# Loading the key cache in 4 KB rows, and the projection weights in pieces, in a decode attention kernel

## Chip, cores and metric

The kernel runs on one core of one Trainium2 chip. The metric is device time in microseconds (us), the median over several executions. Only one core works in every run here, so nothing below says what happens when a second core uses the same memory.

How ratios are computed: a ratio is the mean time of one kernel's runs over the mean of the runs of the kernel before, taken in the same rounds on the same chip. It is therefore not quite the ratio of the medians that are quoted beside it.

Names: TensorE is PE in the profile, its weight load is PEld, VectorE is DVE, ScalarE is ACT, and the engine that only issues transfers is SP. HBM is the memory off the core, SBUF the memory that the engines read, PSUM where TensorE writes. A "row" of a load means bytes that lie back to back both in HBM and in one SBUF partition; the load moves each as one packet.

## The reference

One decode step of attention with grouped heads, over the last W = 512 of 2048 cached keys. B = 32 batch rows, one query each, D = 512, Hq = 32 query heads, Hkv = 8 key/value groups, so 4 query heads per group (rep), head size Dh = 128, everything in bf16.

```python
q = (x @ wq).reshape(B, 1, 32, 128).transpose(0, 2, 1, 3)
k = repeat(k_cache[:, :, -512:, :], 4, axis=1)   # k_cache, v_cache: [32, 8, 2048, 128]
v = repeat(v_cache[:, :, -512:, :], 4, axis=1)
p = softmax(einsum("bhqd,bhkd->bhqk", q, k) * 128 ** -0.5)
o = einsum("bhqk,bhkd->bhqd", p, v)
out = o.transpose(0, 2, 1, 3).reshape(B, 1, 4096) @ wo
```

The part of K that is used is 33.5 MB, that of V as much; wq and wo are 4.2 MB each. Nothing is used twice, so some 75.5 MB must come from HBM once.

## The kernel before

For each of the 8 groups, K of 32 batch rows is loaded and transposed on TensorE (by a matmul with an identity), since the scores need Dh on the partitions. The scores of all 32 batch rows are accumulated into one PSUM tile of 128 rows (32 batch rows x 4 heads) by 512 keys. Then come the softmax, four transposes of P, and the PV matmuls, which are delayed by one group. All loads go through one queue, in program order: K of the next group first, then V of this one.

```python
def issue_k(g):                       # issue_v is the same with v_cache
    kgs = []
    for cb in range(NBCH):            # 4 loads of 8 batch rows, 1 MB each
        kg = kg_pool.tile([P, BCH, NC, Dh], bf16, name="kg", tag="kg")
        dma.dma_start(
            out=kg,
            in_=k_cache[cb * BCH : (cb + 1) * BCH, g, w0:Sk, :].rearrange(
                "b (p c) d -> p b c d", p=P),   # 4 keys (1 KB) per partition and batch row
        )
...
for g in range(Hkv):
    kgs = kg_next
    if g + 1 < Hkv:
        kg_next = issue_k(g + 1)
    vgs = issue_v(g)
    if g == 0:
        wq_h1 = ...; dma.dma_start(out=wq_h1, in_=wq_v[:, :, HHALF * Dh : HD])        # 2 MB
        wo_sb = ...; dma.dma_start(out=wo_sb, in_=wo.rearrange("(h d) n -> d h n", d=P))  # 4 MB
    if g == 2:
        q_proj_heads(wq_h1, HHALF)     # 64 matmuls
    if g >= 3:
        emit_proj(g - 2)               # output projection of an earlier group
    ...
    for b in range(B):
        for c in range(NC):            # NC = 4 transposes of 128 keys
            nc.tensor.matmul(ps_kt[:, c, :], lhsT=kg[:, b % BCH, c, :], rhs=ident, ...)
        ...                            # copy ps_kt to kt, in turn on VectorE and ScalarE
    for b in range(B):
        nc.tensor.matmul(ps_s, lhsT=qp[:, b, :], rhs=kts[b].rearrange("p c pp -> p (c pp)"), ...)
    ...                                # max, exp with sum, reciprocal
    nc.vector.tensor_scalar_mul(out=p_tile, in0=p_tile, scalar1=rs)
    for c in range(NC):
        nc.tensor.transpose(ps_pT[:, c, :], p_tile[:, c, :], ident)
    nc.scalar.copy(out=pT, in_=ps_pT)
    if pending is not None:
        do_pv(*pending)                # 128 matmuls of 4 columns: V stationary, pT moving
    pending = (g, vgs, pT)
do_pv(*pending)
emit_proj(Hkv)
```

## Time and profile before

The median was 230.23 us in four runs (229.79 to 230.33). The profiled span is 228.4 us.

| what | value |
|---|---|
| DMA row of the page | full from the second slice to the third from the end |
| rate in most slices | 345 to 350 GB/s |
| packets under 2 KB | 70,800 of 71,848 |
| one group in TensorE's timeline | 24.1 us |
| wait for the last chunk of V ends | 221.85 us |

From the profile page of the kernel before: the span in 40 slices of 5.7 us. "PEclk" is the clock granted to TensorE and "DMA" the busy share of the 16 DMA engines, both in tenths; "GB/s" is what they moved.

```profile
PEclk9999999985558996799769985999599958996555
DMA  6999999999999999999999999999999999999940
GB/s 192 375 349 349 348 348 348 361 388 350 348 349 348 348 349 348 347 348 348 348 347 346 349 348 348 347 348 346 346 347 350 345 348 349 349 343 345 347 153 6
```

The DMA row is full all along, and the rate stands at one value, about 348 GB/s. It is higher in slices 2, 8 and 9 only, which are the ones with wq, whose rows are 4 KB. The sum 75.5 MB / 348 GB/s is 217 us: the stream of loads is the time, apart from a start and a tail.

From the timeline of the kernel before, TensorE only. The columns are start, length, what ran, how often, and in brackets the idle time before it and what ended that.

```profile
63.55 1.86 PE L118 MATMUL ps_out<-wo_sb,oT_all 128*32 128x512 bf16 x4 [10.14 <-DMA wo_sb<-in_wo_dram]
...
66.55 2.40 PE L201 MATMUL ps_kt<-ident,kg 128*128 128x128 bf16 x20 [1.14 <-DMA kg<-in_k_cache_dram]
...
90.83 2.40 PE L201 MATMUL ps_kt<-ident,kg 128*128 128x128 bf16 x20
...
107.83 1.75 PE L159 MATMUL ps_oT<-pT,vg 128*128 128x4 bf16 x64
110.52 0.38 PE L247 MATMUL ps_pT<-ident,p_tile 128*128 128x128 bf16 x4 [0.94 <-DVE p_tile L243]
...
114.89 1.36 PE L201 MATMUL ps_kt<-ident,kg 128*128 128x128 bf16 x11
...
221.85 1.02 PE L159 MATMUL ps_oT<-pT,vg 128*128 128x4 bf16 x32 [1.79 <-DMA vg<-in_v_cache_dram]
```

TensorE stood for 10.14 us because it needed wo, whose 4 MB sit in the queue behind group 0's V; only at 66.55 us did it begin group 2's transposes. Not needing wo would not have helped by itself: group 2's K lies behind wo in the queue, and after the projection TensorE waits another 1.14 us for it. It was wo's place in the queue that held group 2 up. From there a group takes 24.1 us (114.89 − 90.83), and in it the P transposes wait 0.94 us for the softmax. A group's K and V at 348 GB/s take 24.1 us too, so TensorE and the stream are nearly tied. At the end TensorE waits for the last V chunk until 221.85 us; the last PV matmuls, the last projection, a copy and the store make the tail.

Groups of instructions of the kernel before: busy time and mean length in ns, then the idle time before them.

```profile
L217 PE MATMUL ps_s<-kt,qp 128*128 128x512 bf16 x256 | 76.4, 385 | 0.0
...
L243 DVE TENSOR_SCALAR p_tile<-p_tile,rs 128x512 bf16<-128x512 bf16 x8 | 2.8, 352 | 0.2
```

The scores matmul takes 385 ns and the softmax scaling 352 ns. The view of waits adds that the P transposes wait 6.3 us in total for the scaling.

### The profile page before, as it was taken

What the parts mean: (1) busy time and instruction counts of PE and PEld (TensorE: products, weight loads), DVE (VectorE), ACT (ScalarE), POOL (GpSimd) and SP (SyncE); (2) the same over time, 40 slices, a digit from 0 to 9 for tenths busy, and PEclk for the clock granted to TensorE, in tenths of its full rate; (3) what the DMA queues carried; (4) which work ended last, traced back from release to release, by engine and by line L of the source; (5) the groups of instructions that cost most, each with busy time, mean ns of one, the idle gap of its engine ahead of it and who ended that gap; (6) DMA issues with size and microseconds to landing.
All of it is one profiled execution on the core that took longest, in us unless ns stands there. A gap on an engine that the chain in (4) does not pass through costs nothing.

```text
span 228.4 us, 5681 instructions
## 1 busy us (share of the span) xinstructions
PE 183.4 (80%) x2500; PEld 131.0 (57%) x2500; DVE 106.8 (47%) x205; ACT 86.9 (38%) x153; POOL 0.7 (0%) x6
## 2 busy tenths in 40 slices
PE   0389979983069997999799969998999979995633
PEld 0377657563037765876677556765677557765330
DVE  3068488431026831784258523872188317841001
ACT  2047467410016731573247521761167316732000
POOL 1000000000000000000000000000000000000000
PEclk9999999985558996799769985999599958996555
DMA  6999999999999999999999999999999999999940
GB/s 192 375 349 349 348 348 348 361 388 350 348 349 348 348 349 348 347 348 348 348 347 346 349 348 348 347 348 346 346 347 350 345 348 349 349 343 345 347 153 6
DMA packets 71848, 75.92 MB, mean 332 GB/s; under 512 B 1104, under 2 KB 70800, under 8 KB 71824
## 3 DMA queue, kind: packets, MB, share of 16 engines
q1 hardware_dynamic: 71824, 75.57, 103.3%
q8 instruction: 19, 0.31, 0.6%
q14 instruction: 5, 0.04, 0.1%
HBM read 75.53 MB, written 0.03 MB: 331 GB/s over the span
## 4 chain that ended last, share of the span: by engine, by line
DMA 39%; PE 33%; SPq 20%; ACT 3%; DVE 3%; issue 1%; ACTq 0%
DMA vg<-in_v_cache_dram 21%; SPq L145 17%; PE ps_kt L201 16%; DMA kg<-in_k_cache_dram 15%; PE ps_s L217 10%; PE ps_oT L159 4%; SPq L132 3%; PE ps_out L118 2%; DMA wq_h<-in_wq_dram 2%; ACT kt L212 2%; ACT p_tile L233 1%; DVE rmax L226 1%; PE ps_pT L247 1%; DVE p_tile L243 0%; DVE oT_all L166 0%
## 5 line engine op out<-in xcount | busy, mean ns | idle before, releaser
L210 DVE CAST kt<-ps_kt 128x512 bf16<-128x512 f32 x128 | 87.4, 691 | 44.1 <-PE ps_kt L201 40.6
L212 ACT CAST kt<-ps_kt 128x512 bf16<-128x512 f32 x128 | 74.9, 586 | 80.9 <-PE ps_kt L201 75.8
L201 PE MATMUL ps_kt<-ident,kg 128*128 128x128 bf16 x1024 | 94.3, 233 | 4.7 <-DMA kg<-in_k_cache_dram 2.3
L201 PEld LDWEIGHTS <-kg 128*128 128x128 bf16 x1024 | 77.3, 105 | 34.3 <-issue 9.5
L217 PE MATMUL ps_s<-kt,qp 128*128 128x512 bf16 x256 | 76.4, 385 | 0.0
L159 PE MATMUL ps_oT<-pT,vg 128*128 128x4 bf16 x1024 | 29.9, 165 | 8.6 <-DMA vg<-in_v_cache_dram 8.5
L159 PEld LDWEIGHTS <-vg 128*128 128x128 bf16 x1024 | 29.1, 99 | 11.8 <-DMA vg<-in_v_cache_dram 9.9
L217 PEld LDWEIGHTS <-qp 128*128 128x128 bf16 x256 | 24.3, 99 | 12.9
L118 PE MATMUL ps_out<-wo_sb,oT_all 128*32 128x512 bf16 x32 | 15.1, 626 | 12.8 <-DMA wo_sb<-in_wo_dram 10.1
L226 DVE TENSOR_REDUCE rmax<-ps_s 128x1 f32<-128x512 f32 x8 | 5.5, 691 | 25.0 <-PE ps_s L217 25.0
L233 ACT ACTIVATE p_tile<-ps_s,nbias 128x512 bf16<-128x512 f32 x8 | 5.5, 688 | 29.6 <-DVE nbias L230 29.6
L166 DVE CAST oT_all<-ps_oT 128x128 bf16<-128x128 f32 x8 | 2.3, 292 | 30.7 <-PE ps_oT L159 30.7
L118 PEld LDWEIGHTS <-oT_all 128*32 128x32 bf16 x32 | 3.5, 128 | 17.9 <-issue 14.5
L92 PE MATMUL ps_q<-xT,wq_h 128*128 128x32 bf16 x128 | 3.8, 188 | 6.8 <-DMA wq_h<-in_wq_dram 6.8
L247 PE MATMUL ps_pT<-ident,p_tile 128*128 128x128 bf16 x32 | 3.9, 259 | 6.3 <-DVE p_tile L243 6.3
L249 ACT COPY pT<-ps_pT 128x512 bf16<-128x512 bf16 x8 | 4.7, 587 | 10.3 <-PE ps_pT L247 10.3
L92 PEld LDWEIGHTS <-wq_h 128*128 128x128 bf16 x128 | 3.6, 104 | 7.2 <-DMA wq_h<-in_wq_dram 7.2
L100 DVE CAST qT<-ps_q 128x512 bf16<-128x512 f32 x2 | 1.4, 692 | 11.1 <-PE ps_q L92 11.1
L247 PEld LDWEIGHTS <-p_tile 128*128 128x128 bf16 x32 | 2.4, 111 | 6.8 <-ACT p_tile L233 6.0
L194 DVE COPY qp<-qT 128x32 bf16<-128x32 bf16 x32 | 4.3, 229 | 0.0
L242 DVE RECIPROCAL rs<-rsum 128x1 f32<-128x1 f32 x8 | 1.3, 162 | 4.7 <-ACT p_tile L233 4.7
L243 DVE TENSOR_SCALAR p_tile<-p_tile,rs 128x512 bf16<-128x512 bf16 x8 | 2.8, 352 | 0.2
(14 smaller groups left out, 8.0 us busy)
## 6 DMA issues: line engine op xcount, KB each, us to landing
kg<-in_k_cache_dram SPq DMA_DIRECT2D x32, 1024.0 KB, 11.8
vg<-in_v_cache_dram SPq DMA_DIRECT2D x32, 1024.0 KB, 12.0
wq_h<-in_wq_dram SPq DMA_DIRECT2D x2, 2048.0 KB, 11.0
wo_sb<-in_wo_dram SPq DMA_DIRECT2D x1, 4096.0 KB, 23.4
x_sb<-in_x_dram SPq DMA_DIRECT2D x1, 32.0 KB, 1.7
out_dram<-out_sb SPq DMA_DIRECT2D x1, 32.0 KB, 1.5
```

The source lines that it names most:

```text
L92: nc.tensor.matmul(ps_q[:, hh, :], lhsT=wq_half[:, kc, hl * Dh : (hl + 1) * Dh], rhs=xT[:, kc, :], start=(kc == 0), stop=(kc == KC - 1),)
L118: nc.tensor.matmul(ps_out, lhsT=oT_all[:, h, :], rhs=wo_sb[:, h, :], start=(next_proj[0] == 0), stop=(next_proj[0] == Hq - 1),)
L132: dma.dma_start(out=kg, in_=k_cache[cb * BCH : (cb + 1) * BCH, g, w0:Sk, :].rearrange("b (p c) d -> p b c d", p=P),)
L145: dma.dma_start(out=vg, in_=v_cache[cb * BCH : (cb + 1) * BCH, g, w0:Sk, :].rearrange("b (p c) d -> p b c d", p=P),)
L159: nc.tensor.matmul(ps_oT[:, b * rep : (b + 1) * rep], lhsT=vg[:, b % BCH, c, :], rhs=pT[:, c, b * rep : (b + 1) * rep], start=(c == 0), st ...
L201: nc.tensor.matmul(ps_kt[:, c, :], lhsT=kg[:, b % BCH, c, :], rhs=ident, start=True, stop=True,)
L210: nc.vector.tensor_copy(out=kt, in_=ps_kt)
L212: nc.scalar.copy(out=kt, in_=ps_kt)
L217: nc.tensor.matmul(ps_s, lhsT=qp[:, b, :], rhs=kts[b].rearrange("p c pp -> p (c pp)"), start=(b == 0), stop=(b == B - 1),)
L226: nc.vector.tensor_reduce(out=rmax, in_=ps_s, axis=mybir.AxisListType.X, op=mybir.AluOpType.max)
L233: nc.scalar.activation(out=p_tile.rearrange("r c pp -> r (c pp)"), in_=ps_s, func=AF.Exp, bias=nbias, scale=scale, accum_out=rsum,)
L247: nc.tensor.transpose(ps_pT[:, c, :], p_tile[:, c, :], ident)
```

## The change

It has two intents. The first is longer rows: K is loaded so that a partition holds 16 consecutive keys of one batch row (4 KB) instead of 4 keys (1 KB). A batch row then fills only 32 partitions, so four batch rows share a 512 KB load. Partition n = 4p + b holds keys 16p to 16p + 15 of batch row b. To sort this out again, the transposes use a permutation, `perm`, in place of the identity, and the scores matmul reads its columns in runs of 32 elements (64 bytes). The order of the keys in the scores changes, while V keeps its own layout with 1 KB rows; so the softmax scaling also reorders the columns, with a strided read. The second intent is that TensorE should not wait for weights: the q projection is cut into 16 matmuls per group, and wo comes in eight 512 KB pieces, each queued behind the V of its group.

```diff
+    QB = 4  # batch rows that share the 128 partitions of a K load
+    CQ = NC * QB  # keys (back to back in HBM) per partition: rows of 4 KB
+    perm = const.tile([P, P], bf16, name="perm")
+    nc.vector.tensor_copy(
+        out=perm.rearrange("k (b p) -> k b p", b=QB),
+        in_=ident.rearrange("k (p b) -> k b p", b=QB),
+    )
...  (issue_k)
-            kg = kg_pool.tile([P, BCH, NC, Dh], bf16, name="kg", tag="kg")
-            dma.dma_start(
-                out=kg,
-                in_=k_cache[cb * BCH : (cb + 1) * BCH, g, w0:Sk, :].rearrange(
-                    "b (p c) d -> p b c d", p=P
-                ),
-            )
+            kg = kg_pool.tile([P, BCH // QB, CQ, Dh], bf16, name="kg", tag="kg")
+            for q in range(BCH // QB):
+                b0 = cb * BCH + q * QB
+                kv = k_cache[b0 : b0 + QB, g, w0:Sk, :].rearrange(
+                    "b (p c) d -> p b (c d)", c=CQ
+                )
+                dma.dma_start(
+                    out=kg[:, q].rearrange("p c d -> p (c d)"), in_=kv
+                )
...  (group loop)
+        if g + n_wq_init < Hkv and g % GW == 0:
+            load_wq_wide((g + n_wq_init) // GW)       # 2 MB, 4 KB rows as before
         vgs = issue_v(g)
-        if g == 0:
-            wq_h1 = ...  (2 MB)
-            wo_sb = ...  (4 MB)
-        if g == 2:
-            q_proj_heads(wq_h1, HHALF)
-        if g >= 3:
-            emit_proj(g - 2)
+        wo_pieces[g] = load_wo_piece(g)               # 512 KB
+        if g + 2 < Hkv:
+            q_proj_piece(g + 2, wq_pieces.pop(g + 2)) # 16 matmuls
...  (transposes: rhs=perm instead of rhs=ident)
...  (scores)
-                rhs=kts[b].rearrange("p c pp -> p (c pp)"),
+                rhs=kts[b // QB].rearrange("d c (b p) -> d c b p", b=QB)[:, :, b % QB, :],
...  (softmax scaling)
-        nc.vector.tensor_scalar_mul(out=p_tile, in0=p_tile, scalar1=rs)
+        p_v = work.tile([P, NC, P], bf16, name="p_v", tag="p_v")
+        nc.vector.tensor_scalar_mul(
+            out=p_v.rearrange("r c (p m) -> r c p m", m=QB),
+            in0=p_tile.rearrange("r k n -> r (k n)").rearrange(
+                "r (m c p) -> r c p m", m=QB, c=NC
+            ),
+            scalar1=rs,
+        )
...  (after PV)
             do_pv(*pending)
+            emit_proj(pg, wo_pieces.pop(pg))
```

More of the change, by code (lines that the diff above doesn't have):

```diff
@@ L44 @@
     NBCH = B // BCH
-    HHALF = Hq // 2
-    assert Hkv * rep == Hq and (Hkv // 2) * rep == HHALF
+    QB = 4
+    CQ = NC * QB
+    assert Hkv * rep == Hq
     dma = nc.sync
     const = ctx.enter_context(tc.tile_pool(name="const", bufs=1))
-    wq_pool = ctx.enter_context(tc.tile_pool(name="wq_pool", bufs=1))
-    wo_pool = ctx.enter_context(tc.tile_pool(name="wo_pool", bufs=1))
+    wq_pool = ctx.enter_context(tc.tile_pool(name="wq_pool", bufs=2))
+    wo_pool = ctx.enter_context(tc.tile_pool(name="wo_pool", bufs=4))
     work = ctx.enter_context(tc.tile_pool(name="work", bufs=2))
     kg_pool = ctx.enter_context(tc.tile_pool(name="kg", bufs=6))
-    kt_pool = ctx.enter_context(tc.tile_pool(name="kt", bufs=20))
+    kt_pool = ctx.enter_context(tc.tile_pool(name="kt", bufs=6))
     v_pool = ctx.enter_context(tc.tile_pool(name="v", bufs=2 * NBCH))
@@ L66 @@
     make_identity(nc, ident)
+    perm = const.tile([P, P], bf16, name="perm")
[3 more added lines that the diff above has]
+    )
     x_sb = const.tile([B, D], bf16, name="x_sb")
     dma.dma_start(out=x_sb, in_=x[:, 0, :])
-    wq_v = wq.rearrange("(kc p) n -> p kc n", p=P)
-    wq_h0 = wq_pool.tile([P, KC, HHALF * Dh], bf16, name="wq_h0", tag="wq")
-    dma.dma_start(out=wq_h0, in_=wq_v[:, :, 0 : HHALF * Dh])
     ps_xT = psum_t.tile([P, KC, B], bf16, name="ps_xT", tag="ps_t")
@@ L81, with load_wq_wide, q_proj_piece, load_wo_piece @@
     nc.vector.tensor_copy(out=xT, in_=ps_xT)
+    wq_v = wq.rearrange("(kc p) n -> p kc n", p=P)
+    wo_v = wo.rearrange("(h d) n -> d h n", d=P)
     qT = const.tile([P, Hq, B], bf16, name="qT")
-    HB = 16
-    def q_proj_heads(wq_half, h_start):
-        for hb in range(HHALF // HB):
-            ps_q = psum_s.tile([P, HB, B], fp32, name="ps_q", tag="ps_s")
-            for hh in range(HB):
-                hl = hb * HB + hh
-                for kc in range(KC):
-                    nc.tensor.matmul(
-                        ps_q[:, hh, :],
-                        lhsT=wq_half[:, kc, hl * Dh : (hl + 1) * Dh],
-                        rhs=xT[:, kc, :],
-                        start=(kc == 0),
-                        stop=(kc == KC - 1),
-                    )
-            h0 = h_start + hb * HB
-            nc.vector.tensor_copy(out=qT[:, h0 : h0 + HB, :], in_=ps_q)
-    q_proj_heads(wq_h0, 0)
+    GW = 4
+    def load_wq_wide(w):
+        t = wq_pool.tile([P, KC, GW * rep * Dh], bf16, name="wq_w", tag="wq_w")
+        dma.dma_start(
+            out=t, in_=wq_v[:, :, w * GW * rep * Dh : (w + 1) * GW * rep * Dh]
+        )
+        for i in range(GW):
+            wq_pieces[w * GW + i] = t[:, :, i * rep * Dh : (i + 1) * rep * Dh]
+    def q_proj_piece(g, wq_p):
+        ps_q = psum_s.tile([P, rep, B], fp32, name="ps_q", tag="ps_s")
+        for j in range(rep):
+            for kc in range(KC):
+                nc.tensor.matmul(
+                    ps_q[:, j, :],
+                    lhsT=wq_p[:, kc, j * Dh : (j + 1) * Dh],
+                    rhs=xT[:, kc, :],
+                    start=(kc == 0),
+                    stop=(kc == KC - 1),
+                )
+        nc.vector.tensor_copy(out=qT[:, rep * g : rep * (g + 1), :], in_=ps_q)
+    def load_wo_piece(g):
+        t = wo_pool.tile([P, rep, D], bf16, name="wo_p", tag="wo_p")
+        dma.dma_start(out=t, in_=wo_v[:, g * rep : (g + 1) * rep, :])
+        return t
     oT_all = const.tile([P, Hq, B], bf16, name="oT_all")
@@ L109, with emit_proj @@
     ps_out = psum_out.tile([B, D], fp32, name="ps_out", tag="ps_out")
-    wo_sb = None
-    proj_done = [False] * Hq
     next_proj = [0]
-    def emit_proj(upto_g):
-        for h in range(Hq):
-            if h // rep < upto_g and not proj_done[h]:
-                nc.tensor.matmul(
-                    ps_out,
-                    lhsT=oT_all[:, h, :],
-                    rhs=wo_sb[:, h, :],
-                    start=(next_proj[0] == 0),
-                    stop=(next_proj[0] == Hq - 1),
-                )
-                proj_done[h] = True
-                next_proj[0] += 1
+    def emit_proj(g, wo_p):
+        for j in range(rep):
+            h = rep * g + j
+            nc.tensor.matmul(
+                ps_out,
+                lhsT=oT_all[:, h, :],
+                rhs=wo_p[:, j, :],
+                start=(next_proj[0] == 0),
+                stop=(next_proj[0] == Hq - 1),
+            )
+            next_proj[0] += 1
     def issue_k(g):
@@ L130, in issue_k @@
         for cb in range(NBCH):
-            kg = kg_pool.tile([P, BCH, NC, Dh], bf16, name="kg", tag="kg")
-            dma.dma_start(
-                out=kg,
-                in_=k_cache[cb * BCH : (cb + 1) * BCH, g, w0:Sk, :].rearrange(
-                    "b (p c) d -> p b c d", p=P
-                ),
-            )
+            kg = kg_pool.tile([P, BCH // QB, CQ, Dh], bf16, name="kg", tag="kg")
[3 more added lines that the diff above has]
+                    "b (p c) d -> p b (c d)", c=CQ
+                )
+                dma.dma_start(
+                    out=kg[:, q].rearrange("p c d -> p (c d)"), in_=kv
+                )
             kgs.append(kg)
@@ L169, in do_pv @@
         )
+    WQ_AHEAD = 2
+    n_wq_init = 2 + WQ_AHEAD
+    wq_pieces = {}
+    for g in range(n_wq_init):
+        if g % GW == 0:
+            load_wq_wide(g // GW)
+    for g in range(2):
+        q_proj_piece(g, wq_pieces.pop(g))
     kg_next = issue_k(0)
+    wo_pieces = {}
     pending = None
@@ L176 @@
             kg_next = issue_k(g + 1)
+        if g + n_wq_init < Hkv and g % GW == 0:
+            load_wq_wide((g + n_wq_init) // GW)
         vgs = issue_v(g)
-        if g == 0:
-            wq_h1 = wq_pool.tile([P, KC, HHALF * Dh], bf16, name="wq_h1", tag="wq")
-            dma.dma_start(out=wq_h1, in_=wq_v[:, :, HHALF * Dh : HD])
-            wo_sb = wo_pool.tile([P, Hq, D], bf16, name="wo_sb", tag="wo")
-            dma.dma_start(out=wo_sb, in_=wo.rearrange("(h d) n -> d h n", d=P))
-        if g == 2:
-            q_proj_heads(wq_h1, HHALF)
-        if g >= 3:
-            emit_proj(g - 2)
+        wo_pieces[g] = load_wo_piece(g)
+        if g + 2 < Hkv:
+            q_proj_piece(g + 2, wq_pieces.pop(g + 2))
         for j in range(rep):
@@ L196 @@
         kts = []
-        for b in range(B):
-            kg = kgs[b // BCH]
-            ps_kt = psum_kt.tile([P, NC, P], fp32, name="ps_kt", tag="ps_kt")
-            for c in range(NC):
-                nc.tensor.matmul(
-                    ps_kt[:, c, :],
-                    lhsT=kg[:, b % BCH, c, :],
-                    rhs=ident,
-                    start=True,
-                    stop=True,
-                )
-            kt = kt_pool.tile([P, NC, P], bf16, name="kt", tag="kt")
-            if b % 2 == 0:
-                nc.vector.tensor_copy(out=kt, in_=ps_kt)
-            else:
-                nc.scalar.copy(out=kt, in_=ps_kt)
+        for t in range(B // QB):
+            kg = kgs[t * QB // BCH]
+            kt = kt_pool.tile([P, CQ, P], bf16, name="kt", tag="kt")
+            for i in range(QB):
+                ps_kt = psum_kt.tile([P, NC, P], fp32, name="ps_kt", tag="ps_kt")
+                for c in range(NC):
+                    nc.tensor.matmul(
+                        ps_kt[:, c, :],
+                        lhsT=kg[:, t % (BCH // QB), i * NC + c, :],
+                        rhs=perm,
+                        start=True,
+                        stop=True,
+                    )
+                dst = kt[:, i * NC : (i + 1) * NC, :]
+                if i % 2 == 0:
+                    nc.vector.tensor_copy(out=dst, in_=ps_kt)
+                else:
+                    nc.scalar.copy(out=dst, in_=ps_kt)
             kts.append(kt)
@@ L219 @@
                 lhsT=qp[:, b, :],
-                rhs=kts[b].rearrange("p c pp -> p (c pp)"),
+                rhs=kts[b // QB].rearrange("d c (b p) -> d c b p", b=QB)[
+                    :, :, b % QB, :
+                ],
                 start=(b == 0),
@@ L242 @@
         nc.vector.reciprocal(out=rs, in_=rsum)
-        nc.vector.tensor_scalar_mul(out=p_tile, in0=p_tile, scalar1=rs)
+        p_v = work.tile([P, NC, P], bf16, name="p_v", tag="p_v")
[5 more added lines that the diff above has]
+            scalar1=rs,
+        )
         ps_pT = psum_t.tile([P, NC, P], bf16, name="ps_pT", tag="ps_t")
         for c in range(NC):
-            nc.tensor.transpose(ps_pT[:, c, :], p_tile[:, c, :], ident)
+            nc.tensor.transpose(
+                ps_pT[:, c, :],
+                p_v[:, c, :],
+                ident,
+            )
         pT = work.tile([P, NC, P], bf16, name="pT", tag="pT")
@@ L251 @@
         if pending is not None:
+            pg = pending[0]
             do_pv(*pending)
+            emit_proj(pg, wo_pieces.pop(pg))
         pending = (g, vgs, pT)
+    pg = pending[0]
     do_pv(*pending)
-    emit_proj(Hkv)
+    emit_proj(pg, wo_pieces.pop(pg))
+    assert next_proj[0] == Hq
     out_sb = work.tile([B, D], bf16, name="out_sb", tag="out_sb")
```

## The prediction

> **What bounds the kernel now.** The page's DMA row is full in nearly every slice, at 345 to 350 GB/s; 70,800 of 71,848 packets are under 2 KB. The queue's 75.5 MB take 217 us of the 228.4 us span, so the DMA stream bounds. TensorE is almost tied: in its timeline one group takes 24.1 us from 90.8 to 114.9 us (17 us of transposes and scores, the rest softmax wait, PV and output projection), with no wait for a DMA in it; a group's K plus V, 8.39 MB, takes 24.1 us at 348 GB/s. Earlier TensorE lost 10.1 us waiting for the 4 MB wo (waits view), so group 2 started only at 66.55 us.
>
> **What the change does.** K goes from 1 KB to 4 KB rows; V and wo stay at 1 KB, wq at 4 KB. In the DMA records 1 KB packets take 51 ns, 4 KB ones (wq alone) 159 ns, median. Binned by time, 1 KB rows run at 348 GB/s, and the two bins with wq alone at 407 to 410. The Trainium skill, "DMA: Bandwidth & Descriptors", section "iDMA fabric", has 408.7 GB/s for a lone load stream of 4 KiB rows: they agree. So K's 33.5 MB goes from 96.4 to 82.2 us: 14.2 us less. The last wo piece now queues behind the last V chunk, which lands 1.5 us sooner for that. Off the stream's end: about 15.7 us.
>
> TensorE gains too: no wait for wo, no block of 64 projection matmuls waiting for wq. Group 2 should start near 52 us. Added per group: 16 projection matmuls (0.5 us), and the softmax scaling with a strided read, which should lose its fast rate (352 to about 690 ns, as the 512-column casts take), seen as a longer wait of the P transposes. The scores matmul reads its moving operand in runs of 64 bytes. "SBUF — State Buffer", section on the DMA port swizzle, says consecutive accesses to one 16-byte line run at full bandwidth, so I expect 385 ns unchanged; no run so far shows it.
>
> **Critical path.** From 52 us, six groups of 24.5 us end TensorE's loop near 199 us. The stream lands the last V near 206 us. So it still ends last, by some 6 us, and all of the saving counts. Buffers keep some 20 us of loads ahead. Tail from the last V: 6.5 us, as now. Span about 212.7; the measured time lies 1.8 us above it: **214.5 us**. Range 210 to 221. Chances: faster by over 2% 0.91, within 2% 0.07, slower 0.02.
>
> **What would show each step right.** DMA rate about 400 or more where K moves, 348 where V moves; packets near 48,000; a K packet near 160 ns. Group 2's transposes start near 52 us; no long wait for wo. The scores matmul stays at 385 ns; the scaling rises to 600 to 700 ns. DMA row full until about 206 us; the last PV still waits for V.
>
> **What would make it wrong.** (a) The four batch rows of one K load lie 4 MB apart; if that slows HBM, K gains less (at 380 GB/s only 8 us). (b) If the strided scores read is slower, TensorE takes over: above about 25.5 us a group it bounds the kernel; half rate would add 7 us a group and make it slower than now. (c) The issuing queue waits for TensorE to free K buffers; with TensorE tied, the stream may starve and its row show gaps.

## The result, and the profile after

The changed kernel is correct and takes **214.33 us** (median of 8 runs, 214.19 to 214.59; the kernel before in the same rounds 230.03). The ratio is 0.9319, with an interval of 0.931 to 0.9328. The span fell from 228.4 to 212.7 us.

From the profile page after:

```profile
DMA  5999999999999999999999999999999999999950
GB/s 173 418 410 410 408 407 371 348 358 404 401 350 351 385 407 368 348 358 407 399 347 349 384 406 372 346 359 406 392 352 349 384 406 372 337 343 348 347 189 6
DMA packets 47897, 75.92 MB, mean 357 GB/s; under 512 B 1729, under 2 KB 38657, under 8 KB 47873
```

The rate now has two levels. It is 404 to 418 GB/s in slices where K or wq moves alone and near 348 where V moves alone (down to 337 late in the run), with mixed slices between, and the DMA row is still full throughout.

From the view of chosen windows, first of the kernel before, then of the changed one. The columns are the stretch, its length, the busy time (and count) of PE, PEld, DVE, ACT and POOL, the granted clock, the DMA share, and GB/s. The share can exceed 1, so it is read here only as "full".

```profile
10.00:20.00 10.00, 8.86 (x114) 7.03 (x111) 6.73 (x14) 4.57 (x8) 0.00 (x0) 1.00 1.09 351
...
88.00:94.00 6.00, 5.62 (x55) 3.78 (x52) 2.37 (x4) 1.17 (x2) 0.00 (x0) 0.50 1.10 348
```

```profile
10.00:20.00 10.00, 9.37 (x103) 7.55 (x100) 6.82 (x16) 4.59 (x8) 0.00 (x0) 1.00 1.03 409
36.00:48.00 12.00, 11.99 (x150) 8.01 (x148) 7.35 (x14) 5.90 (x11) 0.00 (x0) 1.00 1.10 353
```

The same ten microseconds, 10 to 20, carry K at 351 GB/s before and at 409 after; V, at 36 to 48 us, still moves at 353. In the DMA records of the trace a 1 KB packet takes 51.4 ns on average before, and after it the 4 KB packets have a median of 161 ns and a mean of 164.7 ns.

TensorE's timeline after:

```profile
52.03 1.89 PE L128 MATMUL ps_out<-wo_p,oT_all 128*32 128x512 bf16 x4 [0.38 <-DVE oT_all L177]
53.85 2.83 PE L222 MATMUL ps_kt<-perm,kg 128*128 128x128 bf16 x28
...
70.05 0.94 PE L170 MATMUL ps_oT<-pT,vg 128*128 128x4 bf16 x32
70.85 0.55 PE L103 MATMUL ps_q<-xT,wq_w 128*128 128x32 bf16 x16
...
72.94 0.40 PE L279 MATMUL ps_pT<-ident,p_v 128*128 128x128 bf16 x4 [0.75 <-DVE p_v L269]
...
75.31 1.60 PE L128 MATMUL ps_out<-wo_p,oT_all 128*32 128x512 bf16 x4 [0.38 <-DVE oT_all L177]
...
143.63 0.40 PE L279 MATMUL ps_pT<-ident,p_v 128*128 128x128 bf16 x4 [1.15 <-DVE p_v L269]
...
194.39 1.87 PE L128 MATMUL ps_out<-wo_p,oT_all 128*32 128x512 bf16 x4 [0.42 <-DMA wo_p<-in_wo_dram]
...
206.10 1.02 PE L170 MATMUL ps_oT<-pT,vg 128*128 128x4 bf16 x32 [1.77 <-DMA vg<-in_v_cache_dram]
```

Group 2's transposes start at 53.85 us instead of 66.55, and no wait for wo is over 0.42 us. The projection lines show a group's length, 75.31 − 52.03 = 23.3 us; those of the later groups are up to 23.7, and the last is 24.7 with a wait of 0.79 us for V in it. TensorE finishes the projection of group 6 at 196.3 us and then meets the remaining V chunks one by one: the last wait ends at 206.10 us instead of 221.85. Those 15.75 us are the whole gain (the span fell by 15.7 us); the tail from there is 6.6 us in both kernels.

Groups of instructions after, answering to those shown before:

```profile
L239 PE MATMUL ps_s<-kt,qp 128*128 128x512 bf16 x256 | 74.3, 382 | 0.0
...
L269 DVE TENSOR_SCALAR p_v<-p_tile,rs 128x512 bf16<-128x512 bf16 x8 | 5.2, 650 | 0.2
```

The scores matmul with 64-byte runs takes 382 ns against 385. The scaling takes 650 ns instead of 352, yet the P transposes wait 6.4 us in total against 6.3. The timeline shows why: in the first four of seven groups the 16 matmuls of the q projection (at 70.85 us) run while the softmax is at work, and the wait is 0.75 us. The last three have no q projection left, and there it is 1.08 to 1.15 us, longer than the 0.94 of before.

### The profile page after: what moved, and what is told of

It is laid out like the page before. It is cut to its first block, busy times and chain, and to the rows that moved or that the text cites. A ratio compares the mean times of both kernels' runs of the same rounds, so it can differ in the third digit from the quotient of the medians.

```text
span 212.7 us, 5631 instructions
## 1 busy us (share of the span) xinstructions
PE 181.5 (85%) x2500; PEld 130.7 (61%) x2500; DVE 109.0 (51%) x212; ACT 86.8 (41%) x153; POOL 0.7 (0%) x6
## 2 busy tenths in 40 slices
DMA packets 47897, 75.92 MB, mean 357 GB/s; under 512 B 1729, under 2 KB 38657, under 8 KB 47873
## 4 chain that ended last, share of the span: by engine, by line
PE 35%; DMA 31%; SPq 26%; DVE 4%; ACT 2%; issue 1%
SPq L156 20%; PE ps_kt L222 17%; DMA kg<-in_k_cache_dram 16%; PE ps_s L239 12%; DMA vg<-in_v_cache_dram 12%; SPq L114 4%; DMA wq_w<-in_wq_dram 4%; PE ps_out L128 3%; SPq L146 2%; PE ps_oT L170 2%; ACT p_tile L257 1%; DVE kt L231 1%; DVE rmax L250 1%; PE ps_q L103 1%; DVE p_v L269 1%
## 5 line engine op out<-in xcount | busy, mean ns | idle before, releaser
L231 DVE CAST kt<-ps_kt 128x512 bf16<-128x512 f32 x128 | 86.5, 690 | 31.7 <-PE ps_kt L222 28.1
L222 PE MATMUL ps_kt<-perm,kg 128*128 128x128 bf16 x1024 | 94.1, 233 | 1.9 <-ACT kt L233 0.9
L239 PE MATMUL ps_s<-kt,qp 128*128 128x512 bf16 x256 | 74.3, 382 | 0.0
L128 PE MATMUL ps_out<-wo_p,oT_all 128*32 128x512 bf16 x32 | 14.8, 615 | 3.1 <-DVE oT_all L177 2.7
L103 PE MATMUL ps_q<-xT,wq_w 128*128 128x32 bf16 x128 | 4.3, 181 | 6.4 <-DMA wq_w<-in_wq_dram 6.4
L279 PE MATMUL ps_pT<-ident,p_v 128*128 128x128 bf16 x32 | 3.5, 240 | 6.4 <-DVE p_v L269 6.4
L103 PEld LDWEIGHTS <-wq_w 128*128 128x128 bf16 x128 | 3.9, 99 | 6.7 <-DMA wq_w<-in_wq_dram 6.5
L279 PEld LDWEIGHTS <-p_v 128*128 128x128 bf16 x32 | 2.0, 104 | 7.0 <-DVE p_v L269 7.0
L110 DVE CAST qT<-ps_q 128x128 bf16<-128x128 f32 x8 | 2.3, 289 | 7.7 <-PE ps_q L103 7.7
L269 DVE TENSOR_SCALAR p_v<-p_tile,rs 128x512 bf16<-128x512 bf16 x8 | 5.2, 650 | 0.2
```

What stands on the lines that cost most here:

```text
L103: nc.tensor.matmul(ps_q[:, j, :], lhsT=wq_p[:, kc, j * Dh : (j + 1) * Dh], rhs=xT[:, kc, :], start=(kc == 0), stop=(kc == KC - 1),)
L128: nc.tensor.matmul(ps_out, lhsT=oT_all[:, h, :], rhs=wo_p[:, j, :], start=(next_proj[0] == 0), stop=(next_proj[0] == Hq - 1),)
L222: nc.tensor.matmul(ps_kt[:, c, :], lhsT=kg[:, t % (BCH // QB), i * NC + c, :], rhs=perm, start=True, stop=True,)
L231: nc.vector.tensor_copy(out=dst, in_=ps_kt)
L239: nc.tensor.matmul(ps_s, lhsT=qp[:, b, :], rhs=kts[b // QB].rearrange("d c (b p) -> d c b p", b=QB)[:, :, b % QB, :], start=(b == 0), stop ...
L269: nc.vector.tensor_scalar_mul(out=p_v.rearrange("r c (p m) -> r c p m", m=QB), in0=p_tile.rearrange("r k n -> r (k n)").rearrange("r (m c ...
```

## The experiments

Theory A, that of the prediction: the DMA stream ends last in both kernels. The longer rows of K give some 14 us and the position of the last wo piece the rest; the earlier start of TensorE only keeps it off the end. Rival B: TensorE was the tied partner, and most of the gain comes from removing its 10 us wait. Then one asks what the next step on the stream would give, and where TensorE takes over.

### Splitting the weights alone

```diff
 (changed kernel)
-    QB = 4
+    QB = 1        # K as before: 1 MB loads with 1 KB rows; the rest of the change stays
```

> The changed kernel with K loaded and used as before (1 KB rows), wq and wo still in the new pieces. Theory 'stream' (the load stream ends last and only its bytes per row count): all rows but wq's are 1 KB again, so about 228 to 229 us, 1 to 1.5 us under the kernel before, because the last V chunk no longer queues behind wo. Rival 'waits' (the gain came from TensorE no longer waiting 10.1 us for wo): about 216 us, most of the gain. Group 2's transposes should start earlier than 66.5 us in both.

Measured: 228.5 us (228.34 to 228.91; before 229.88), ratio 0.9937 (0.992 to 0.9953). TensorE's timeline of this run:

```profile
56.13 2.40 PE L220 MATMUL ps_kt<-perm,kg 128*128 128x128 bf16 x20 [1.09 <-DMA kg<-in_k_cache_dram]
...
220.52 1.01 PE L168 MATMUL ps_oT<-pT,vg 128*128 128x4 bf16 x32 [1.77 <-DMA vg<-in_v_cache_dram]
```

Group 2 starts at 56.13 us, 10.4 us earlier than before, and the time moves by 1.4 us. The last V lands 1.3 us earlier (221.85 to 220.52): that is about what the 512 KB of wo, now behind it, take at 348 GB/s (1.5 us). Rival B falls: ten microseconds of TensorE's wait are worth nothing while the stream ends last.

### Longer rows of K alone

```diff
 (changed kernel)
-        wo_pieces[g] = load_wo_piece(g)
-        if g + 2 < Hkv:
-            q_proj_piece(g + 2, wq_pieces.pop(g + 2))
+        if g == 0:
+            (wq_h1, 2 MB, and wo_sb, 4 MB, loaded as in the kernel before)
+        if g == 2:
+            q_proj_heads(wq_h1, HHALF)
+        if g >= 3:
+            emit_proj(g - 2)
...  (the projection after each PV is gone; K stays in 4 KB rows)
```

> The kernel before with K alone in 4 KB rows; wq in halves and wo in one 4 MB load as before. Theory 'stream': about 215.8 us (230.0 less 14.2). Rival 'waits': 228 to 230 us. A mixture (each half needs the other): 219 to 224 us, with TensorE's loop ending after the last V load has landed.

Measured: 215.81 us (215.64 to 216.22), ratio 0.9389 (0.9375 to 0.9403). TensorE's timeline:

```profile
59.81 1.44 PE L127 MATMUL ps_out<-wo_sb,oT_all 128*32 128x512 bf16 x3 [9.01 <-DMA wo_sb<-in_wo_dram]
...
207.25 1.01 PE L170 MATMUL ps_oT<-pT,vg 128*128 128x4 bf16 x32 [0.19 <-DMA vg<-in_v_cache_dram]
```

The wait for wo is back at 9.01 us, and the time is only 1.5 us above the changed kernel. The last wait for V is 0.19 us, though: TensorE reached the end just as V did. The rows give the time; the splitting gives the slack that would have been used up here.

### Rows of 2 KB, and small loads with 1 KB rows

```diff
-    QB = 4
+    QB = 2        # two batch rows share the partitions: 2 KB rows, 256 KB loads
```

> The changed kernel with two batch rows per K load instead of four: rows of 2 KB. If a row costs a fixed part plus its bytes, a line through 47.1 ns (1 KB at 348 GB/s over 16 engines) and 160 ns (4 KB at 409) gives 84.8 ns, 386 GB/s: K takes 86.9 us instead of 82.2, so 4.7 us above the changed kernel, about 219 us. If only the largest rows help (a step), it stays near 228; if 2 KB is already enough, near 214.5. Packets: 16,384 of 2 KB.

Measured: 225.71 us (223.34 to 228.43; one of four runs is over 1.5% above the fastest), ratio 0.9783 (0.972 to 0.9846). This is a miss of some 6 us, and by the 2% limit the verdict against the kernel before is unclear. The four runs scatter by 5 us. In the DMA records the median 2 KB packet takes 85 ns, close to the 86 that a straight line through the medians of the changed kernel gives (49 ns for 1 KB, 161 ns for 4 KB), but the mean is 89.3 ns. Two stretches from the window view, an early and a late one:

```profile
22.00:26.00 4.00, 4.00 (x34) 2.33 (x31) 1.84 (x3) 1.81 (x4) 0.00 (x0) 1.00 1.05 386
...
178.00:182.00 4.00, 4.00 (x26) 2.51 (x25) 1.38 (x2) 1.17 (x2) 0.00 (x0) 0.50 0.88 289
```

The early stretch runs as expected, at 386 GB/s with the engines full. In the late one the DMA share is 0.88 and the rate 289 GB/s, while TensorE is busy. One suspect was the 256 KB load, so the next run kept 1 KB rows and used it:

```diff
 (weights-split kernel, K with 1 KB rows)
-            dma.dma_start(out=kg, in_=k_cache[cb * BCH : (cb + 1) * BCH, g, w0:Sk, :]...)
+            for q in range(BCH // 2):
+                b0 = cb * BCH + 2 * q      # two batch rows, 256 KB, 1 KB rows
+                dma.dma_start(out=kg[:, 2 * q : 2 * q + 2], in_=k_cache[b0 : b0 + 2, g, w0:Sk, :]...)
```

> The split-only kernel (K in 1 KB rows) with K in loads of 256 KB instead of 1 MB: the rows and their number are unchanged. In the 2 KB run, packets took what the line says (85 ns, median) but the engines' busy share fell to 0.80 to 0.97 in K's stretches. Theory 'small loads': at most eight loads are in flight, 2 MB of K then, and the queues run dry: here too the share falls below 1.05 in K's stretches, the time rises above 228.5 (to 231 to 236) and scatters by more than 1%. Rival '2 KB rows themselves, or batch rows 4 MB apart': 228.5 us, unchanged, scatter as before.

Measured: 228.77 us (228.68 to 229.03; before 230.04), ratio 0.9947 (0.9932 to 0.9962), with no scatter. Small loads by themselves cost next to nothing at 1 KB rows, so that suspect, taken alone, falls. Why the 2 KB run loses its 6 us stays open.

### Rows of 8 KB, and what is wrong with them

```diff
-    QB = 4
+    QB = 8        # eight batch rows share the partitions: 8 KB rows, 1 MB loads
```

> The changed kernel with eight batch rows per K load: rows of 8 KB, one 1 MB load each. The same line gives 311 ns for 8 KB, 421 GB/s, if such a row is one packet: K takes 79.6 us, 2.6 us less, about 211.8 us. If it is cut into two packets of 4 KB, or the rate has reached its ceiling: about 214.5 us, unchanged. TensorE's own work grows little (runs of 32 bytes in the scores matmul); if that read slows down, its mean rises above 382 ns and the time rises.

Measured: 285.98 us (281.82 to 293.25; two of four runs over 1.5% above the fastest), ratio 1.2283 (1.2252 to 1.2313). This was the largest miss. From its page:

```profile
GB/s 238 273 229 224 227 229 297 364 348 255 235 222 334 330 239 242 268 350 285 264 248 330 321 255 268 260 348 263 259 234 284 337 225 238 225 314 339 329 301 12
```

K moves at 222 to 273 GB/s, and an 8 KB packet takes 546 ns on average in the DMA records. Two things differ from the 4 KB kernel: the packet's size and the layout, in which the 128 partitions of a load fall on eight batch rows, 16 partitions each. Two runs take them apart. The first keeps the layout and halves the packet:

```diff
 (8 KB kernel)
-                dma.dma_start(out=kg[:, q]..., in_=kv)
+                for h in range(2):     # half of each row per load: 4 KB packets
+                    dma.dma_start(out=kg[:, q, h * 16 : (h + 1) * 16]...,
+                                  in_=kv[:, :, h * 16 * Dh : (h + 1) * 16 * Dh])
```

> The layout of the 8 KB run (eight batch rows to a load, 16 partitions each), but each 8 KB row is moved in two loads of 4 KB rows. Theory 'addresses' (with eight batch rows, 4 MB apart, several of them are read at once by different DMA engines): 4 KB packets of K take about half of the 546 ns of an 8 KB one, 230 to 280 ns, instead of 164, and the time stays above 250 us. Rival 'packet size' (a packet over 4 KB is slow): 4 KB packets take 164 ns and the time is near that of the changed kernel, 214 to 217 us.

Measured: 272.5 us (272.0 to 276.5; one of four runs over 1.5% above the fastest), ratio 1.1842 (1.1814 to 1.1869). Its page:

```profile
GB/s 227 291 252 248 245 245 316 355 350 249 253 247 349 323 258 268 291 349 290 280 267 346 319 268 295 264 346 239 239 241 286 344 255 310 275 341 347 340 211 8
DMA packets 47895, 75.91 MB, mean 281 GB/s; under 512 B 1728, under 2 KB 38656, under 8 KB 47872
```

The packet count is the changed kernel's, and the slowness stays: a 4 KB packet takes 248 ns on average instead of 164.7. The second run keeps the changed kernel's K and gives wq 8 KB rows, which lie back to back:

```diff
-    GW = 4  # KV groups per wq load: rows of GW KB
+    GW = 8
```

> The changed kernel with wq in one 4 MB load of 8 KB rows, which lie back to back in memory. Theory 'addresses': these 8 KB packets take about 311 ns (the line through 1 KB and 4 KB). Rival 'packet size': about 546 ns, as K's did. The time matters little: TensorE starts some 5 us later, which its slack of 7 us should hide: 214 to 216 us.

Measured: 213.92 us in a single look (state unknown; span 212.1). The 8 KB packets of wq have a median of 309 ns, where the same straight line says 310. So packets of 8 KB are not slow as such. The layout with eight batch rows is, and it is so with 4 KB packets too. Whether it is the addresses in HBM (the batch rows lie 4 MB apart), or how the 16 engines share such a load, no run tells.

### Longer rows of V too, as a look at the stream alone (wrong result on purpose)

```diff
 (issue_v of the changed kernel)
-            dma.dma_start(out=vg, in_=v_cache[cb * BCH : (cb + 1) * BCH, g, w0:Sk, :]...)
+            for q in range(BCH // QB):     # 4 KB rows as K; PV uses them as if nothing had changed
+                b0 = cb * BCH + q * QB
+                dma.dma_start(
+                    out=vg[:, q * QB : (q + 1) * QB].rearrange("p b c d -> p (b c d)"),
+                    in_=v_cache[b0 : b0 + QB, g, w0:Sk, :].rearrange("b (p c) d -> p b (c d)", c=CQ))
```

> The changed kernel with V loaded in 4 KB rows too and everything else as it is, so the result is wrong on purpose (V's keys and batch rows are mixed up); the work of every engine is unchanged. Theory 'stream, then TensorE': the stream gets another 14.2 us shorter and would land the last V near 192 us, but TensorE's loop of 23.6 us a group then ends last: its six groups from 52 us end near 194 to 196 us, plus PV of the last group and the tail; span 203 to 205, about 205 us, and TensorE no longer waits for V at the end. Rival 'stream alone': the full 14.2 us, about 200 us. Rival 'V's rows do not matter': 214.3 us.

Measured: 206.05 us (204.23 to 207.1; before 230.07), ratio 0.8944 (0.8887 to 0.9). The result is wrong, since V's rows meet the wrong columns of P; no arithmetic was added. From TensorE's timeline at the end:

```profile
195.46 3.57 PE L172 MATMUL ps_oT<-pT,vg 128*128 128x4 bf16 x128
```

The whole last PV, 128 matmuls, runs without a wait for V. The DMA row of the page ends one slice earlier than in the changed kernel, and the slices are shorter (5.12 us against 5.32). So when the stream gains a further 14 us by estimate, the kernel gets 8: TensorE takes over as the one that ends last.

### More work on TensorE

```diff
 (transposes)
-                for c in range(NC):
+                for c in [0] * (4 if i == 0 else 0) + list(range(NC)):  # 32 repeats a group
```

> The changed kernel with 32 transposes a group done over again (same place, same value, correct result): 1.8 us more TensorE work a group at 56 ns each, up to 3.4 us where the clock is halved; over eight groups 14 to 27 us. Theory 'stream ends last with TensorE 6 to 7 us behind': the time grows by the added work less that slack: 7 us more at the least, 221 to 235 us, with TensorE no longer waiting for the last V. If TensorE already set the pace, all of it shows: 228 us or more with waits for V gone before as well. If TensorE were far from mattering: 214.3 us.

Measured: 218.68 us (218.36 to 219.17), ratio 0.9511 (0.9495 to 0.9527); the result is right. A group now takes 25.0 to 25.8 us. TensorE's timeline at the end:

```profile
205.86 1.89 PE L128 MATMUL ps_out<-wo_p,oT_all 128*32 128x512 bf16 x4 [0.38 <-DVE oT_all L177]
207.68 3.57 PE L170 MATMUL ps_oT<-pT,vg 128*128 128x4 bf16 x128
```

The projection of group 6 starts at 205.86 us against 194.39, so TensorE lost 11.5 us; the span grew by 4.2. The difference, some 7.3 us, is the slack that TensorE has in the changed kernel: that much added work was free. The run before gives a like figure: there TensorE waits for no V at the end, and its span of 204.6 us is 8.1 us below the changed kernel's 212.7. As in the run before, no wait for V is left at the end. The repeats cost less than I had expected, so the time is below the range.

### Longer rows of V, done right

V in 4 KB rows puts four batch rows on the partitions of one V chunk. A PV matmul then contracts over keys of four batch rows at once, so P must be transposed into that layout with zeros where the query's batch row is not the partition's. That takes 16 P transposes per group instead of 4, the scaling writes P four times over, and the copy out of PSUM multiplies with a mask. The number of PV matmuls stays 128, with 16 columns instead of 4.

```diff
+        p_v = pv_pool.tile([P, CQ // 2, PK, QB], ...)       # two halves; P repeated for each b
...
+            for cc in range(CQ // 2):                        # 8 transposes a half
+                nc.tensor.transpose(ps_pT[:, cc, :], p_vs[h][:, cc].rearrange("r p b -> r (p b)"), ident)
+            nc.vector.tensor_tensor(out=pT[:, half h], in0=ps_pT, in1=mask, op=mult)
...
+            for c in range(CQ):
+                nc.tensor.matmul(ps_oT[:, t * QR : (t + 1) * QR],           # QR = 16
+                                 lhsT=vg[:, t % (BCH // QB), c, :],
+                                 rhs=pT[:, c, t * QR : (t + 1) * QR], ...)
```

> V in 4 KB rows with a correct result: partition p*4+b of V holds batch row b, so P is repeated for the four b before its transposes (sixteen of them instead of four a group) and masked in the copy out of PSUM; the PV matmuls are as many as before, 16 columns wide instead of 4. The stream is that of the run before this one. TensorE has 12 transposes more a group, 0.7 to 1.3 us by the 56 to 107 ns that a transpose takes at the two clocks, so six groups add 4 to 8 us to the TensorE-bound time of the wrong-result run: about 210 us. 'Stream alone' says about 200 us. If the added VectorE work (about 2.3 us a group) or the longer wait for P shows, 212 to 216.

Measured: 217.18 us (215.77 to 217.86), ratio 0.9436 (0.94 to 0.9472); correct, and slower than the changed kernel. One group in TensorE's timeline:

```profile
129.11 1.89 PE L142 MATMUL ps_out<-wo_p,oT_all 128*32 128x512 bf16 x4 [0.38 <-DVE oT_all L196]
...
150.11 0.62 PE L308 MATMUL ps_pT<-ident,p_v 128*128 128x128 bf16 x8 [1.25 <-DVE p_v L298]
...
153.75 1.89 PE L142 MATMUL ps_out<-wo_p,oT_all 128*32 128x512 bf16 x4 [0.39 <-DVE oT_all L196]
```

The projections lie 24.6 us apart here (153.75 − 129.11), some 25.1 us on average over the groups, against 23.5. In the middle, the P transposes wait 1.25 us for the scaling and, in a line left out, 0.40 us for the masked copy. The stream is done some 24 us before the end: its page shows 0, 3, 3 and 6 GB/s in the last four slices. TensorE decides now, and what it lacks is work to do while it waits for the softmax.

### The same, with the waiting work queued later

```diff
             for t in range(B // QB):  (K transposes of the next group)
+                if t >= 1 and deferred:
+                    with tc.issue_after(last_kt.ins):
+                        deferred.pop(0)()
...
-            do_pv_part(ps_oT, pvgs, ppT, 0, 4); p_half(0)
-            do_pv_part(ps_oT, pvgs, ppT, 4, 8); p_half(1)
-            emit_proj(pg, wo_pieces.pop(pg))
+            do_pv_part(ps_oT, pvgs, ppT, 0, 8)
+            deferred = [projection, p_half(0), p_half(1)]    # between the next K transposes
```

> K and V in 4 KB rows with a correct result, and TensorE's loop made shorter: P's transposes and the four output projections of a group are queued behind K transposes of the next group instead of standing right after PV, where TensorE waits 0.8 to 1.2 us for P and 0.4 us for PV's copy and runs at half clock. If TensorE's loop was what kept the last two V runs from 200 us, it now takes about 21.6 us a group (23.6 less 1.2, 0.4 and 1.0, plus 0.5 for 12 more transposes at full clock), less than the stream's 22.0 (8.39 MB at 409 GB/s, wo at 348), so the stream ends last again: last V near 192 us, about 200 us in all, up to 206 if the added copies slow the K stage. If the loop does not get shorter, 214 to 217 as in the run with V in 4 KB rows before it.

Measured: **201.12 us** (200.78 to 201.25; before 230.04), ratio 0.8741 (0.8728 to 0.8754); correct. This is the best kernel. From its page:

```profile
PEclk9999999999999999999999979999999999997555
GB/s 162 409 416 406 411 410 406 409 400 400 406 408 405 393 407 407 409 397 402 410 405 408 391 410 406 412 393 402 406 409 400 396 411 405 410 394 407 372 127 7
```

From TensorE's timeline:

```profile
76.28 1.04 PE L142 MATMUL ps_out<-wo_p,oT_all 128*32 128x512 bf16 x4
...
98.10 1.04 PE L142 MATMUL ps_out<-wo_p,oT_all 128*32 128x512 bf16 x4
...
192.70 0.59 PE L187 MATMUL ps_oT<-pT,vg 128*128 128x16 bf16 x16 [0.67 <-DMA vg<-in_v_cache_dram]
```

A group takes 21.8 us (98.10 − 76.28; the five gaps between projections of this kind are 21.4 to 22.6), and the four projection matmuls 1.04 us instead of 1.89, which goes with the full clock in the PEclk row. Of the 3.3 us by which a group is shorter than in the run before (25.1 against 21.8), the three waits seen there make 2.0 us (1.25, 0.40 and 0.39) and the faster projection 0.85, so the gain is not that of the filled waits alone. The rate is about 400 GB/s or more in nearly every slice, and the stream ends last again, by a little: the last three V chunks are waited for 0.63 to 0.67 us each, and the last wo piece 0.77 us.

### Queuing later alone

```diff
 (changed kernel, V in 1 KB rows as it has it; K transposes of the next group:)
+            if t >= 1 and deferred:
+                with tc.issue_after(last_kt.ins):
+                    deferred.pop(0)()
 (after the softmax)
-            emit_proj(pg, wo_pieces.pop(pg))
+            deferred.append(lambda pg=pg: emit_proj(pg, wo_pieces.pop(pg)))
+        deferred.append(p_all)      # the four P transposes and their copy
```

> The changed kernel (K in 4 KB rows, V in 1 KB rows) with TensorE's loop made shorter as in the run before: P's transposes and the output projections queued behind the next group's K transposes. TensorE's loop should fall from 23.6 to about 21.5 us a group, but the stream still ends last and is untouched: about 214 us, within 1 us of the changed kernel, with TensorE waiting for K or V in every group. If TensorE's loop sets part of the time, it is faster by 2 us or more.

Measured: 214.64 us (214.27 to 214.92; before 229.86), ratio 0.9342 (0.9327 to 0.9358). TensorE's timeline:

```profile
94.98 1.79 PE L170 MATMUL ps_oT<-pT,vg 128*128 128x4 bf16 x64
98.14 1.97 PE L223 MATMUL ps_kt<-perm,kg 128*128 128x128 bf16 x16 [1.38 <-DMA kg<-in_k_cache_dram]
...
146.88 3.25 PE L223 MATMUL ps_kt<-perm,kg 128*128 128x128 bf16 x28 [1.76 <-DMA kg<-in_k_cache_dram]
...
205.86 1.01 PE L170 MATMUL ps_oT<-pT,vg 128*128 128x4 bf16 x32 [1.81 <-DMA vg<-in_v_cache_dram]
```

TensorE runs through its work sooner and then stands before the next group's K, 1.76 us in the line shown; the last wait for V ends where it did. The granted clock does not stay up here, though the waits for P are filled as in the run before. From the page:

```profile
PEclk9999999998899759995599969995899759995555
```

It still falls once a group. By the clock record of the trace one fall comes at 95.98 us, inside PV (which ends at 96.77 us) and before the wait for K of 1.38 us; TensorE had had no idle time since 89.74 us. So filled waits alone do not keep the clock up, and what does so in the 201.12 us kernel is not shown. The four corners are:

| | P work and projection in place | both queued later |
|---|---|---|
| V in 1 KB rows | 214.33 | 214.64 |
| V in 4 KB rows | 217.18 | 201.12 |

Either step alone gives nothing or less; together they give 13 us. The faster stream is not worthless by itself: in the run with the wrong result it gave 8 us (206.05), and the work on TensorE that makes it correct took them back.

## Why the prediction was right, point by point

The time was right, 214.5 us predicted and 214.33 measured, and the reason held.

- **The stream bounds the kernel.** Shown: with only the weights split, TensorE's start moves by 10.4 us and the time by 1.4 us; with only the rows, the time falls by 14 us.
- **Rates of 348 and some 408 GB/s, packets near 160 ns.** The windows show 353 and 409, the records a median of 161 ns. From the rates, 33.5 MB of K save 14.2 us; the rows-alone run moves the last V by 14.6 us (221.85 to 207.25). Packets: 47,897, predicted near 48,000. The agreement with the Trainium skill's 408.7 GB/s, which the prediction named, holds for K as well.
- **1.5 us from the order of wo behind V.** The split-alone run moves the last V by 1.3 us.
- **The last V near 206 us, tail 6.5 us.** 206.10 us, and 6.6 us.
- **Worry (a), four batch rows 4 MB apart.** It did not come true with four, where K has its full 409 GB/s. With eight batch rows to a load the rate collapsed.
- **Worry (b), the scores matmul with 64-byte runs.** It did not come true: 382 ns against 385. This agrees with what the prediction took from "SBUF — State Buffer".
- **Worry (c), the stream starving.** The DMA row shows no gap.
- **The scaling at 600 to 700 ns.** It is 650, so the fast rate is lost. The Trainium skill, "VectorE: DVE Perf Modes", section "What auto-detection actually checks", accounts for a part of that: packing two elements into one read needs a step of 1 or −1. For using both read ports the same section asks for no such step, only for outermost dimensions that are even or equal, which these operands have; but 650 ns is near the 691 ns of the 512-column casts and shows no such gain. Why it is missing is not shown. The prediction's remark that the slower scaling would be seen as a longer wait of the P transposes held only where no q projection fills it (1.15 us against 0.94, at 143.63 us); in total that wait is 6.4 us against 6.3. From the end of the scores to the P transposes the timeline does show 2.9 us (70.05 to 72.94) instead of 2.7 (107.83 to 110.52), but there the q projection fills part of it, so the wait is 0.75 us.
- **Group 2's start near 52 us.** It was 53.85.
- **The term that was mis-sized: TensorE's groups of 24.5 us, ending near 199 us.** They took 23.3 to 23.7 us (the last one 24.7, with a wait for V), and TensorE's loop ended at 196.3 us, 9.8 us before the last V (206.10) instead of "some 6". Some PV work still lies in between; the run with more work puts the slack itself at about 7.3 us. The step that failed took the 24.1 us of a group as a fixed sum of work and added to it. From the window view, the stretch of transposes and scores of one group before, and of two groups after:

```profile
90.83:107.83 17.00, 16.86 (x161) 12.05 (x161) 10.92 (x16) 9.38 (x16) 0.00 (x0) 0.89 1.10 348
```

```profile
53.85:70.05 16.20, 16.08 (x162) 11.33 (x161) 10.82 (x16) 9.38 (x16) 0.00 (x0) 0.96 1.08 364
76.84:93.23 16.39, 16.33 (x162) 11.69 (x161) 10.80 (x16) 9.38 (x16) 0.00 (x0) 0.93 1.07 366
```

The same matmuls take 17.00 us at a granted clock of 0.89 before, and 16.20 and 16.39 us at 0.96 and 0.93 after. Length times clock is nearly the same (15.1, 15.6 and 15.2 us). So the 0.6 to 0.8 us that a group was shorter in this stretch goes with a higher granted clock, which the prediction had not looked at. Why the clock was higher is not shown. The q projection between PV and the P transposes is not enough of a reason: the stretches from 147.92 and 171.54 us come after groups without it and take 16.46 and 16.59 us at 0.91. By the clock records the half clock, apart from the last stretch of a run, lasts 3.41 us or a multiple of it, 6.83 us in the group shown before and 3.41 us in each of the two shown after, and how much of that falls on the transposes differs from group to group. The rest of a group, from PV to the projection, took 7.06 us before and 6.8 to 7.4 us after, so that the 0.5 us of the q projection did not come on top in full. The error did no harm, since TensorE had slack in either case. A first explanation of mine, that TensorE waited for K at the start of a group, fell: the timeline of weight loads does put a gap of 0.84 us there down to K before the change, but the same 0.84 us stands there after it without that label.

## What to carry to other kernels

When the DMA row is full, cost the row length of the loads from the packet times in the trace before counting anything that TensorE would save, and then find by one run with added work how much slack the second engine has, because the next step on the stream will run into it. Two changes that did nothing alone here, a faster stream that brings TensorE more work and a tighter TensorE under a slow stream, were worth 13 us together, so test the pair. A group's time on TensorE is no fixed sum either: the same matmuls took 17.0 us or 16.2 us as the granted clock changed.

## What the Trainium skill lacked or had wrong

- "DMA: Bandwidth & Descriptors", section "Bandwidth", gives measured rates by the size of a transfer. On the length of a row it has a fixed overhead per packet, worked out for 256 bytes, and no rate for rows of 1 to 8 KB. Here the row decides: 1 KB rows run at 348 GB/s in loads of 1 MB and of 256 KB alike, 4 KB rows at 409 in loads of 512 KB, and back-to-back 8 KB rows take 309 ns a packet, which over 16 engines is an estimate of 424 GB/s.
- The same page's note on row pitch in HBM ("Latency and other measured facts") tells of slow copies at pitches of 2 to 8 MiB, 103 GB/s at 4 MiB. Batch rows here lie 4 MB apart. Four of them in a load run at 409 GB/s, while eight, in 8 KB rows, run at 222 to 273, and in 4 KB rows their packets take 248 ns against 164.7. The page does not say how many such streams a load may have; whether it is the same mechanism is not shown.
- No page explains the 2 KB rows: the median packet is as expected (85 ns), but the rate falls to 289 GB/s late in the run, with a DMA share of 0.88, and the times scatter by 5 us.
- "TensorE: Matmul & The Clock Gate", Part 1, ties the half clock to an idle window of about 3.4 us; its section on a second failure mode speaks of short idles, without a length. In the kernel before, at 88 to 94 us, the granted clock is 0.50 while TensorE is busy 5.62 of 6.00 us, and the longest idle time near by is 0.94 us. Idle time is not even needed: with P and the projection queued later alone, the clock falls at 95.98 us after 6 us without any, and in the 201.12 us kernel, whose row of the granted clock is 9 in nearly every slice, it falls once at 116.69 us after 3.6 us without any. In both cases PV was running (matmuls of 4 or 16 columns); whether that is the cause is not shown.
